# A conditioned transformer block on one core: gate vectors formed as columns and spread later, the last tile's output in three pieces, and a new order of all work

## The chip, the cores and the metric

The kernel runs on one core of a Trainium2 chip. A core has five engines with an instruction queue each: TensorE (PE, matmuls and transposes, writing to PSUM), VectorE (DVE), ScalarE (ACT), GpSimd (POOL) and SyncE (SP, which here issues DMAs). Each takes its instructions in the order in which they were written; between engines, semaphores hold an instruction back until its inputs are there. The metric is device time in microseconds (us), the median over runs of the whole program.

## What is computed

The block has an attention half A and a feed-forward half B. A conditioning vector `c` gives six modulation vectors of 512 numbers each: shifts `sa`, `sb`, scales `ca`, `cb` and gates `ga`, `gb`.

```python
mod = (_silu(c) @ w_mod).reshape(c.shape[0], 6, 1, -1)
sa, ca, ga, sb, cb, gb = (mod[:, 0], mod[:, 1], mod[:, 2], mod[:, 3], mod[:, 4], mod[:, 5])
h = _layernorm(x, axis=-1) * (1 + ca) + sa
x = x + ga * _A_ref(h, A_wqkv, A_w_phi, A_wo)
h = _layernorm(x, axis=-1) * (1 + cb) + sb
x = x + gb * _B_ref(h, B_w_gate, B_w_up, B_w_down)
```

`x` is 2048 tokens of 512 numbers in bf16. `_A_ref` is linear attention with 32 heads of width 16: q and k go through a small matrix per head, and `softmax(p)` and `softmax(-p)` side by side are the features; keys and values are summed to one small matrix per head, and each query reads it. `_B_ref` is `(silu(x @ w_gate) * (x @ w_up)) @ w_down` with a width of 1376.

## The kernel before

The tokens are 16 tiles of 128, in four chunks of four tiles. The work runs in these stages, which overlap:

- **Start.** SP loads x chunk by chunk and the weights. DVE takes layernorm statistics (`bn_stats`, line 348). The key weight is folded with the head matrices: PE transposes it (519), ACT copies the result from PSUM (523), PE multiplies (530) with the block matrix `BD` (made by DVE, 502), and ACT or DVE copy the folded weight back (533, 534). The shift and scale columns `modA` come from one-column matmuls against `w_mod` (473).
- **Keys and values.** Normalized tiles `xn` are turned to columns and modulated to `hT`. Tiles 0 to 5 are turned by PE (563, 414) with ACT or DVE modulating from PSUM (566, 567, 422); from tile 6 on by a DMA transpose into `raw` (577, called raw10 and raw11 by buffer), with POOL, ACT or DVE modulating (587, 589). For each tile, `k_tile` has PE compute k (619) and v (623), ACT exponentiate (634), DVE sum (640), and POOL multiply the second half of the features (657). `kv_tile` accumulates keys against values in PSUM (663). After the last one, DVE writes the matrix `KVZ`.
- **Queries.** `q_tile`: PE (686), ACT exponentials (690), DVE sums (694), POOL products (697, 701), and a DMA transpose into `pT` (705).
- **Attention.** `attend_tile` reads `pT` against `KVZ` (806), DVE divides (809, 810), a transpose gives `oT` (829 by DMA), `project` multiplies with `wo` (839), DVE adds to x (842), and the second layernorm follows: POOL (359 to 362), normalize, a DMA transpose into `raw` (853), and modulation to `hT` by DVE, ACT or POOL (860, 862, 864).
- **Feed-forward.** It runs in units of 1, 1, 2, 4, 4 and 4 tiles: gate and up products (891), silu on ACT (898), the product on DVE (901) or through ACT and POOL (905, 907), a narrow tail of 96 features (937 to 946), and `ffn_down` (969). The down product is multiplied by `gb` (980), added to x (984) and sent out by SP (989).

The gates `ga` and `gb` must stand as rows, the same on all 128 partitions, in `gab`. `gate` makes them in one step: for each quarter of the conditioning vector, PE takes one column of `silu(c)`, broadcast to 128 columns, as the stationary operand and streams 512 columns of `w_mod` (718); ACT copies the result from PSUM (721). `ga` is multiplied into `wo` by POOL (762). The variable `turned` marks the place from which the buffers of the first half may be used anew; it waits for `gab`, among others, and the first `attend_tile` waits for it.

The last tile's output is made in two halves of 256 columns. The first goes the usual way. The second uses `wdg`, the down weight with `gb` already multiplied in (916), so that after PE only one DVE operation (976) and the output DMA, which ACT issues, remain.

Nothing in this order is left to a scheduler. Every piece of work is recorded by `pl.op` with the engines that may do it, a duration for planning, and what it reads and writes. `ORDER` is a list written out by hand: each number is four times the number of an operation plus the choice of its engine. `Plan.run` goes through this list, works out a planned start for each operation from the durations, and issues all instructions sorted by that start. Where PE would be without work in the plan, `fill` puts in matmuls of ones whose result nobody reads (1036). `Plan.DMA` holds the plan's constants for DMAs; its last is the planned time from the end of a DMA transpose's transfer until its data count as there. Buffers in PSUM are six banks, given out in the planned order.

Of the kernel before, what the change touches and what calls it, by code (L numbers as in the profile page):

```python
# [7 lines left out]
BF16 = mybir.dt.bfloat16  # L8
FP32 = mybir.dt.float32
ACT = mybir.ActivationFunctionType  # L10
# [4 lines left out]
P = 128  # L15
# [5 lines left out]
D = 512  # L21
# [14 lines left out]
def fm_size(m):  # L36
# [10 lines left out]
    0, 4, 80, 72, 8, 12, 16, 48, 228, 188, 60, 204, 76, 20, 84, 89, 52, 220, 64, 192, 172, 208, 224, 232, 156, 160, 196, 164, 92, 56, 98, 236, 201,  # L47
    240, 244, 176, 212, 104, 108, 24, 100, 112, 248, 168, 216, 180, 116, 120, 148, 184, 153, 124, 132, 128, 276, 260, 28, 268, 40, 316, 272, 136,
    140, 280, 144, 324, 252, 520, 68, 488, 36, 285, 256, 424, 320, 328, 264, 288, 294, 298, 428, 524, 472, 464, 560, 600, 308, 432, 32, 476, 532,
    332, 564, 336, 300, 342, 44, 528, 480, 436, 468, 312, 608, 492, 368, 346, 484, 497, 380, 440, 445, 304, 568, 536, 541, 452, 604, 448, 572, 404,  # L50
    460, 500, 768, 372, 456, 548, 544, 612, 348, 556, 577, 376, 776, 392, 510, 584, 864, 408, 772, 358, 396, 617, 353, 366, 828, 780, 624, 832, 804,
    412, 812, 400, 820, 596, 362, 808, 552, 620, 416, 580, 513, 785, 792, 872, 904, 384, 636, 506, 518, 1004, 816, 824, 592, 388, 868, 876, 940,
    1008, 944, 836, 588, 640, 908, 704, 840, 708, 1012, 788, 912, 644, 632, 797, 1016, 648, 880, 860, 420, 628, 800, 916, 858, 712, 958, 900, 962,
    988, 950, 1044, 1021, 953, 888, 921, 853, 850, 1292, 1028, 736, 892, 716, 928, 740, 1024, 924, 964, 884, 846, 1172, 1288, 1312, 1328, 1176,
    1212, 652, 1216, 896, 720, 933, 1252, 656, 936, 1184, 1256, 1040, 744, 1220, 1344, 1180, 1224, 660, 1036, 1264, 664, 1189, 1336, 992, 1192,
    1229, 1196, 1297, 1320, 1260, 1208, 1302, 1236, 1032, 1306, 1309, 1340, 748, 1204, 1348, 1248, 1504, 1269, 1232, 1800, 1544, 1508, 1272, 1241,
    1276, 1244, 1201, 1353, 1584, 1588, 1356, 1281, 752, 1332, 1360, 968, 1592, 1516, 1284, 724, 1596, 1368, 1548, 1556, 1624, 972, 1372, 1512,
    1521, 1052, 1365, 668, 1552, 1524, 1528, 1540, 756, 1628, 976, 1536, 1601, 1636, 1561, 728, 1533, 980, 1604, 1580, 1641, 1608, 1048, 1108, 1564,
    1613, 1316, 1632, 1568, 1648, 1056, 1116, 1620, 1112, 1616, 1076, 1573, 672, 1644, 1576, 1660, 1808, 1653, 1120, 1080, 1656, 760, 676, 1812,
    1816, 996, 984, 680, 684, 732, 1000, 1324, 1820, 1728, 1840, 1844, 1084, 1060, 1736, 1848, 1088, 1092, 1664, 1140, 2148, 2152, 2156, 1796, 1672,  # L60
    1804, 1792, 1732, 1148, 1064, 1852, 764, 1856, 688, 1144, 1068, 1376, 1096, 1860, 1100, 2160, 1072, 1760, 1864, 2164, 1380, 1696, 1668, 1104,
    2168, 1868, 1764, 1472, 1872, 2400, 1700, 1440, 1152, 2404, 692, 1768, 2408, 1384, 1480, 1476, 696, 1408, 1876, 2412, 2172, 1882, 1704, 1124,
    1128, 2416, 1156, 1160, 700, 1884, 1892, 2200, 2420, 1896, 1164, 1888, 2176, 1132, 2204, 1996, 2208, 1920, 2180, 2212, 2424, 2184, 2216, 1444,
    2188, 1940, 1448, 1416, 2192, 1412, 2000, 1136, 1900, 1388, 2004, 2221, 1948, 1928, 1936, 1956, 1964, 1924, 1168, 2428, 1944, 2198, 1420, 2496,
    2008, 1932, 2224, 2452, 2012, 1960, 1952, 1904, 2237, 1424, 2500, 2016, 2504, 1428, 1908, 2432, 1392, 2508, 2456, 2242, 2020, 2436, 1484, 2440,
    2230, 1972, 2024, 2028, 1976, 2233, 2320, 2268, 1432, 1436, 2328, 2264, 2032, 2512, 2300, 1912, 2516, 1772, 2272, 1396, 2280, 2460, 2920, 1968,
    2037, 2316, 2336, 2288, 2324, 1488, 1400, 2284, 1916, 2520, 2924, 2276, 2040, 1776, 2292, 1492, 2308, 1980, 1496, 1404, 2548, 2044, 2244, 2048,
    2332, 1500, 1708, 2928, 2464, 2344, 2444, 1712, 2552, 2052, 2248, 2908, 2468, 2252, 2912, 2340, 2072, 2524, 2474, 1452, 2256, 1456, 2556, 2108,
    2088, 2916, 2449, 2560, 1984, 2296, 2564, 2528, 2116, 2932, 1460, 2476, 2112, 2092, 2120, 2376, 3016, 2532, 1465, 2076, 2100, 1468, 2536, 1676,
    2348, 3020, 2260, 2540, 2569, 1716, 2304, 2080, 1680, 2056, 2312, 2545, 2060, 2490, 3024, 2096, 2352, 1720, 1740, 2936, 2482, 2960, 2064, 3004,  # L70
# [50 lines left out]

class Plan:


    HOP = {"PE": 0.23, "DVE": 0.18, "ACT": 0.2, "POOL": 0.14, "SP": 0.0, "XBAR": 0.08, "NONE": 0.0}
    OWN = {"PE": 0.0, "DVE": 0.14, "ACT": 0.16, "POOL": 0.12, "SP": 0.0, "XBAR": 0.0, "NONE": 0.0}
    DMA = (1.7, 385e3, 0.5, 0.6, 1.15, 0.8)
    LANES = 8

    def __init__(self, slots):  # L130
        self.ops = []
        self.slots = slots
        self.queue, self.sent = 0.7, [2.5]
# [942 lines left out]
```

## Time and profile before

| quantity | value |
|---|---|
| time, median of 3 runs | 200.48 us (200.48 to 200.94) |
| the profiled execution | 200.42 us, of which the span of the profile is 198.6 us |
| granted TensorE clock | 1.00 |
| PE busy in the span | 193.3 us, 1450 matmuls |
| filler matmuls (L1036) | 25, all before 16 us |
| gate matmuls (L718) | 8 of 512 columns, the first at 30.5 us, the last group at 53.9 us |
| copies to gab (L721) | 2 of 0.576 us mean, at 38.4 and 54.8 us |
| first attend group (L806) | 55.59 us |
| DMA transposes, issue to landing, median | pT 3.3, raw 3.2, oT 3.3, gut 2.3 us |

PE is called busy from a matmul's start to its modelled end, so a busy PE can hide short waits; the starts of matmuls that follow each other are the better measure. A row of a timeline gives start, length, engine, line and operation, with idle time before it and what ended it in square brackets. A row of a group gives busy time and the mean of one. In the chain of waits each row is a stretch of the path that ended last. "issue" in it is time in which nothing that the profile shows was waited for.

### The profile page before, as it was taken

How to read it: one execution, taken by the hardware profiler on the slowest of the kernel's cores; microseconds unless marked ns; L12 is line 12 of the kernel's file. 1: busy time of each engine (PE TensorE's matmuls, PEld its weight loads, DVE VectorE, ACT ScalarE, POOL GpSimd, SP SyncE). 2: the span in 40 equal slices, each digit the busy share in tenths (PEclk: the TensorE clock that was granted, in tenths of full speed). 3: DMA queues.
4: the chain of work that ended last, by engine and by line, in shares of the span. 5: the costliest groups of instructions: out<-in, count | busy, mean ns of one | idle time of the engine just before them, and what ended most of it. 6: DMA issues, size and time to landing. Idle time of an engine off the chain costs nothing.

```text
span 198.6 us, 3986 instructions
## 1 busy us (share of the span) xinstructions
PE 193.3 (97%) x1450; PEld 107.4 (54%) x1450; DVE 138.2 (70%) x274; ACT 110.7 (56%) x243; POOL 122.5 (62%) x201
## 2 busy tenths in 40 slices
PE   7999999999999999999999999999999999999993
PEld 2755555456545776878644544544444454444542
DVE  4999999999999999979889728563305502214363
ACT  2799999998787973573334545454234444311200
POOL 1539999999997765783780487634272261962620
PEclk9999999999999999999999999999999999999999
DMA  6999877799798595544798333300311210020022
GB/s 203 345 392 142 237 121 213 177 360 314 183 194 165 109 154 31 112 80 59 144 189 80 71 68 79 83 0 13 79 27 42 79 53 0 13 70 1 26 92 66
DMA packets 50997, 24.16 MB, mean 122 GB/s; under 512 B 42177, under 2 KB 47778, under 8 KB 50978
## 3 DMA queue, kind: packets, MB, share of 16 engines
q1 hardware_dynamic: 50832, 23.85, 51.9%
q8 instruction: 11, 0.18, 0.4%
q10 hardware_dynamic: 146, 0.07, 0.1%
q14 instruction: 8, 0.07, 0.1%
HBM read 11.58 MB, written 2.10 MB: 69 GB/s over the span
## 4 chain that ended last, share of the span: by engine, by line
PE 84%; DMA 6%; POOL 3%; DVE 2%; SPq 1%; issue 1%; ACT 1%; DVEq 0%
PE one_ps L891 29%; PE one_ps L969 16%; PE one_ps L623 7%; PE one_ps L686 7%; PE one_ps L619 7%; PE one_ps L839 4%; PE kv_ps L1036 4%; DMA raw<-xn 3%; PE one_ps L937 2%; DMA pT<-eq 2%; PE kv_ps L663 2%; PE kv_ps L806 2%; PE one_ps L530 1%; PE one_ps L718 1%; PE one_ps L473 1%
## 5 line engine op out<-in xcount | busy, mean ns | idle before, releaser
L891 PE MATMUL one_ps<-hT,wgu_sb 128*128 128x512 bf16 (+2 forms) x480 | 74.5, 308 | 0.3 <-ACT hT L862 0.3
L891 PEld LDWEIGHTS <-wgu_sb 128*128 128x128 bf16 x480 | 39.9, 98 | 27.5 <-issue 0.6
L898 ACT ACTIVATE sg<-one_ps 128x512 bf16<-128x512 f32 (+1 forms) x41 | 23.5, 585 | 34.4 <-PE one_ps L891 31.4
L969 PE MATMUL one_ps<-wd_sb,gu 128*128 128x512 bf16 (+1 forms) x160 | 37.5, 372 | 0.0
L907 POOL TENSOR_TENSOR gu<-usb,sg 128x512 bf16<-128x512 bf16 x19 | 21.7, 1153 | 16.9 <-ACT sg L898 16.6
L980 DVE TENSOR_TENSOR fg<-one_ps,gab 128x512 bf16<-128x512 f32 (+1 forms) x16 | 10.7, 670 | 24.0 <-PE one_ps L969 24.0
L969 PEld LDWEIGHTS <-gu 128*128 128x128 bf16 x170 | 16.3, 98 | 16.8
L348 DVE BATCH_NORM_STATS2 st<-x_c 128x6 f32<-128x512 bf16 x32 | 20.9, 680 | 1.7 <-DMA x_c<-in_A_x_dram 1.7
L905 ACT CAST usb<-one_ps 128x512 bf16<-128x512 f32 x19 | 11.0, 583 | 16.1 <-PE one_ps L891 15.6
L901 DVE TENSOR_TENSOR gu<-one_ps,sg 128x512 bf16<-128x512 f32 (+1 forms) x22 | 14.3, 655 | 7.9 <-PE one_ps L891 5.4
L640 DVE TENSOR_REDUCE S<-e 128x64 f32<-128x1024 bf16 x16 | 19.0, 1204 | 0.3 <-POOL e L657 0.3
L694 DVE TENSOR_REDUCE Sq<-eq 128x64 f32<-128x1024 bf16 x16 | 19.1, 1199 | 0.0
L690 ACT ACTIVATE eq<-one_ps 128x512 bf16<-128x512 f32 x32 | 17.3, 608 | 1.5 <-PE one_ps L686 1.4
L984 POOL TENSOR_TENSOR ot<-x_c,fg 128x512 bf16<-128x512 bf16 x9 | 10.3, 1151 | 12.0 <-DVE fg L980 5.0
L657 POOL TENSOR_TENSOR e<-e,S 128x512 bf16<-128x512 bf16 x16 | 16.9, 1065 | 0.2
L634 ACT ACTIVATE e<-one_ps 128x512 bf16<-128x512 f32 x32 | 17.0, 600 | 0.0
L359 POOL TENSOR_SCALAR ln_neg<-ln 128x1 f32<-128x1 f32 x16 | 3.5, 220 | 20.7 <-DVE ln L349 20.1
L839 PE MATMUL one_ps<-wo_sb,oT 128*128 128x512 bf16 x64 | 15.8, 379 | 0.0
L619 PE MATMUL one_ps<-wk,hT 128*128 128x512 bf16 x64 | 15.4, 379 | 0.0
L623 PE MATMUL one_ps<-wv,hT 128*128 128x512 bf16 x64 | 15.4, 379 | 0.0
L686 PE MATMUL one_ps<-wq,hT 128*128 128x512 bf16 x64 | 15.3, 379 | 0.0
L701 POOL TENSOR_TENSOR eq<-eq,Rq 128x512 bf16<-128x512 bf16 x14 | 14.7, 1058 | 0.6
(117 smaller groups left out, 283.1 us busy)
## 6 DMA issues: line engine op xcount, KB each, us to landing
wmod_sb<-in_w_mod_dram SPq DMA_DIRECT2D x2, 1024.0 KB, 5.6
out_dram<-ot SPq DMA_DIRECT2D x15, 128.0 KB, 1.9
x_c<-in_A_x_dram SPq DMA_DIRECT2D x3, 512.0 KB, 7.5
wgu_sb<-in_B_w_up_dram SPq DMA_DIRECT2D x1, 1376.0 KB, 7.4
wgu_sb<-in_B_w_gate_dram SPq DMA_DIRECT2D x1, 1376.0 KB, 9.3
wd_sb<-in_B_w_down_dram SPq DMA_DIRECT2D x1, 1280.0 KB, 7.9
wk<-in_A_wqkv_dram SPq DMA_DIRECT2D x1, 512.0 KB, 4.5
wmod_sb<-in_w_mod_dram SPq DMA_DIRECT2D x1, 512.0 KB, 6.0
```

Source lines behind the costliest of these rows:

```text
L348: pl.op("DVE", r=reads, w=[st6], us=0.6, fn=lambda: nc.vector.bn_stats(st6()[:], src))
L619: nc.tensor.matmul(pk()[:], lhsT=hT[c_i][k][:, cols], rhs=Wk2[:, k, :], start=(k == 0), stop=(k == KD - 1))
L623: nc.tensor.matmul(v()[:], lhsT=hT[c_i][k][:, cols], rhs=wv_sb[:, k, :], start=(k == 0), stop=(k == KD - 1))
L640: pl.op("DVE", r=[e], w=[Ss], us=1.13, fn=lambda: nc.vector.tensor_reduce(Ss()[:].rearrange("p g s h -> p (g s h)"), e()[:].rearrange("p g ...
L686: nc.tensor.matmul(pq()[:], lhsT=hT[c_i][k][:, cols], rhs=Wq2[:, k, :], start=(k == 0), stop=(k == KD - 1))
L690: pl.op("ACT", r=[pq, btab], w=[be[sg]], us=0.48, fn=lambda sg=sg: nc.scalar.activation(eq[:, :, sg].rearrange("p g h f -> p g (h f)"), pq ...
L694: pl.op("DVE", r=be, w=[Sq], us=1.13, fn=lambda: nc.vector.tensor_reduce(Sq()[:].rearrange("p g s h -> p (g s h)"), eq[:].rearrange("p g s ...
L839: nc.tensor.matmul(a()[:], lhsT=oT()[:, j0 + j, :], rhs=wo_sb[:, j, :], start=(j == 0), stop=(j == KD - 1))
L891: nc.tensor.matmul(ps_()[0:fsz, q * n:(q + 1) * n], lhsT=wgu_sb[:, k, i, m * P:m * P + fsz], rhs=h2[k], start=(k == 0), stop=(k == KD - 1))
L898: pl.op("ACT", r=[g, btab], w=[sg], us=0.08 + 0.41 * L / CW, fn=lambda: nc.scalar.activation(sg()[0:fsz, 0:L], g()[0:fsz, 0:L], ACT.Silu))
L907: pl.op("POOL", r=[usb, sg], w=[gu], us=0.17 + 0.98 * L / CW, fn=lambda: nc.gpsimd.tensor_tensor(gu()[0:fsz, 0:L], usb()[0:fsz, 0:L], sg() ...
L969: nc.tensor.matmul(fp()[:], lhsT=b()[0:fsz, c0:c0 + P], rhs=wd_[0:fsz, m, wcs], start=(m == 0), stop=(m == FM - 1))
```

## The change

Four things change.

First, the gates are made in two steps. `gate` now makes each of its 512 numbers as a column: for each of four quarters of `c` and each of four blocks of 128 outputs, a one-column matmul with a block of `w_mod` as the stationary operand. The result is 128 partitions by 4 columns and is copied to `gcol`. `spread_gate` then makes the row form: each of four columns, broadcast to 128 columns, is the stationary operand, and the identity is streamed; the copy to `gab` follows, on ACT or DVE. `turned` waits for `gcol` instead of `gab`.

Second, the last tile's output is made in three pieces: 256, 128 and 128 columns. The second and third use `wdg`; SP sends the second and ACT the third.

Third, the plan's last DMA constant goes from 0.8 to 1.1.

Fourth, `ORDER` is a new list (the numbers of operations shift too, as there are more of them). With it, engines change for some operations: two of four WT copies (523) go from ACT to DVE, five normalizations from DVE to POOL, two from ACT to POOL and one from ACT to DVE, the statistics of chunk 2 from POOL to ACT, and others. On SP's queue, the loads of `wd` now stand before and between the transposes of chunk 2 and chunk 3 (raw11, raw10), and the second half of `w_mod` behind the latter. Lines after 712 move by 18.

```diff
 ORDER = [
-    0, 4, 80, 72, 8, 12, 16, 48, 228, 188, 60, 204, 76, 20, 84, 89, 52, 220, 64, 192, 172, 208, 224, 232, 156, 160, 196, 164, 92, 56, 98, 236, 201,
...
+    0, 4, 48, 188, 72, 80, 8, 12, 16, 76, 20, 60, 52, 204, 228, 84, 56, 220, 172, 64, 208, 89, 92, 98, 156, 232, 176, 224, 24, 212, 104, 180, 193,
...
-    DMA = (1.7, 385e3, 0.5, 0.6, 1.15, 0.8)
+    DMA = (1.7, 385e3, 0.5, 0.6, 1.15, 1.1)
...
+    gcol = const.tile([P, 2, KD], BF16, name="gcol")
+    bgcol = [Buf(), Buf()]
+
     def gate(gi):
-        col0 = (2 * D, 5 * D)[gi]
-        t = bank("fold")
+        n0 = (2 * KD, 5 * KD)[gi]
+        t = bank("fold", [P, KD])
 
         def f():
             for k in range(KD):
-                nc.tensor.matmul(t()[:], lhsT=silucT[:, k:k + 1].to_broadcast([P, P]), rhs=wmod_sb[:, k, col0:col0 + D],
-                                 start=(k == 0), stop=(k == KD - 1))
-        pl.op("PE", r=[bsil, bm2[gi]], w=[t], us=0.865, fn=f)
-        pl.op("ACT", r=[t], w=[bgab[gi]], us=0.49, fn=lambda: nc.scalar.copy(gab[:, gi, :], t()[:]))
+                for n in range(KD):
+                    nc.tensor.matmul(t()[:, n:n + 1], lhsT=wmod_sb[:, k, (n0 + n) * P:(n0 + n + 1) * P], rhs=silucT[:, k:k + 1],
+                                     start=(k == 0 and n == 0), stop=(k == KD - 1), skip_group_check=True)
+        pl.op("PE", r=[bsil, bm2[gi]], w=[t], us=0.42, fn=f)
+        pl.op([("DVE", 0.13, lambda: nc.vector.tensor_copy(gcol[:, gi, :], t()[:])),
+               ("ACT", 0.12, lambda: nc.scalar.copy(gcol[:, gi, :], t()[:]))], r=[t], w=[bgcol[gi]])
+
+    def spread_gate(gi):
+        t = bank("fold")
+
+        def f():
+            for n in range(KD):
+                nc.tensor.matmul(t()[:, n * P:(n + 1) * P], lhsT=gcol[:, gi, n:n + 1].to_broadcast([P, P]), rhs=ident_b[:],
+                                 start=True, stop=True)
+        pl.op("PE", r=[bgcol[gi]], w=[t], us=0.23, fn=f)
+        pl.op([("ACT", 0.49, lambda: nc.scalar.copy(gab[:, gi, :], t()[:])),
+               ("DVE", 0.6, lambda: nc.vector.tensor_copy(gab[:, gi, :], t()[:]))], r=[t], w=[bgab[gi]])
...
             gate(1)
+            spread_gate(0)
+            spread_gate(1)
...
-    turned = pl.op("NONE", r=bKVZ + bgab + [bmodB, bmodA] + bWq2, w=[bturn], us=0.0, fn=f_turn)
+    turned = pl.op("NONE", r=bKVZ + bgcol + [bmodB, bmodA] + bWq2, w=[bturn], us=0.0, fn=f_turn)
...
-        nh = 2 if n == NT - 1 else 1
-        for h in range(nh):
-            cs = slice(h * D // nh, (h + 1) * D // nh)
-            fp = bank("down", (P, D // nh))
+        pieces = [(0, D // 2), (D // 2, 3 * D // 4), (3 * D // 4, D)] if n == NT - 1 else [(0, D)]
+        for c0, c1 in pieces:
+            cs, cw, h = slice(c0, c1), c1 - c0, int(c0 > 0)
+            fp = bank("down", (P, cw))
...
-            q = nc.scalar if h == 1 else nc.sync
-            pl.op("ACT" if h == 1 else "XBAR", r=[ot], us=0.45, kb=-1,
+            on_act = c1 == D and h == 1
+            q = nc.scalar if on_act else nc.sync
+            pl.op("ACT" if on_act else "XBAR", r=[ot], us=0.45, kb=-1,
```

## The prediction

> **What bounds the kernel now.** I read the page's head first, then busy time by stretch, then the chain of waits, then the instructions of TensorE (PE) in order of time, and last the end of the run.
>
> ```profile
> span 198.6 us, 3986 instructions
> ...
> PE 193.3 (97%) x1450; PEld 107.4 (54%) x1450; DVE 138.2 (70%) x274; ACT 110.7 (56%) x243; POOL 122.5 (62%) x201
> ```
>
> PE is busy throughout, so the time is PE's own work plus what it loses. The loss has four places: the start, two waits in the middle, and the end. By stretch (columns: length, PE, weight loads, DVE, ACT, POOL, clock, DMA share, GB/s):
>
> ```profile
> 20.00:30.00 10.00, 10.00 (x75) 5.28 (x74) 10.00 (x20) 9.81 (x26) 9.92 (x19) 1.00 0.80 175
> 30.00:40.00 10.00, 10.00 (x75) 4.91 (x74) 9.95 (x13) 9.87 (x27) 9.78 (x17) 1.00 0.75 202
> 40.00:50.00 10.00, 10.00 (x117) 5.89 (x116) 9.65 (x12) 8.90 (x28) 10.00 (x19) 1.00 0.96 326
> ```
>
> From 20 to 50 us every engine is full: PE has no wait there, but whatever DVE, ACT or POOL deliver late would reach it at once. The two waits in PE's own timeline, and the links of the chain of waits in front of them:
>
> ```profile
> 77.00 4.53 PE L891 MATMUL one_ps<-hT,wgu_sb 128*128 128x256 bf16 x40
> 81.83 0.43 PE L806 MATMUL kv_ps<-KVZ,pT 128*128 128x68 bf16 x8 [0.30 <-DMA pT<-eq]
> ...
> 101.77 0.38 PE L891 MATMUL one_ps<-hT,wgu_sb 128*128 128x512 bf16 x1
> 102.43 0.81 PE L891 MATMUL one_ps<-hT,wgu_sb 128*128 128x512 bf16 x3 [0.28 <-ACT hT L862]
> ```
>
> ```profile
> 71.91 3.25 DMA raw<-xn
> ...
> 77.39 4.40 DMA pT<-eq
> ...
> 97.48 3.29 DMA raw<-xn
> 100.80 1.59 ACT hT L862 x3
> ```
>
> Matmul ends are modelled, so I price these two by starts. A 256-column matmul takes 0.108 us in a run (40 make 4.33), so L806 was due at 81.33 and began at 81.83: 0.50 lost. A 512-column one takes 0.2155 (0.86 for four in the chain), so from 98.74, fourteen of L969 and one of L891 end at 101.98; the next began at 102.43: 0.45. Together 0.95 us. The end:
>
> ```profile
> 195.29 0.33 SPq L989 DMA_DIRECT2D out_dram<-ot  x1
> 195.38 0.42 DVE L976 TENSOR_TENSOR ot<-one_ps,x_c 128x256 bf16<-128x256 f32 x1
> 195.83 0.38 ACTq L989 DMA_DIRECT2D out_dram<-ot  x1
> ```
>
> PE ends about 195.33, DVE at 195.80; the ACT piece lands 1.7 us after its issue (197.5), SP's last tile 1.9 after its own (197.2).
>
> **What the Trainium skill says.** "TensorE: Matmul & The Clock Gate", section "Wait — 56ns, not 53.3ns?", puts a floor of about 25 ns under start-to-start of small matmuls; here sixteen one-column L473 take 0.38 us in the chain and twenty-four 0.68, 24 to 28 ns each: it agrees. "DMA: Bandwidth & Descriptors", "Queues, rings and completion order", says that an SDMA engine takes the descriptors of a row in ring order, so a transpose issued behind a large load waits for it. The trace is consistent: SP's transposes and loads all sit on queue q1, and none is shown overtaking. "VectorE: DVE Perf Modes", "The perf-mode tier table", caps a copy out of PSUM at 2x; no row of before has DVE copying bf16 out of PSUM.
>
> **The change, part by part.**
>
> *Gates.* Two groups of four 512-column matmuls (L718) go: 2 x 0.86 = -1.72. Thirty-two one-column matmuls at 26 ns come: +0.83. Two spreads of four 128-column matmuls (0.22 per four, L414 in the chain): +0.44. Sum -0.45 on PE, which is the bound. Beside it come two tiny copies to gcol, bounded by nothing and by the 0.17 us of the modA copy (L478), on an ACT that also loses two WT copies; the gab copies stay (0.576 each). The turn no longer waits for gab: in before L806's first group began at 55.59, after gab ended at about 55.38, so that wait was already no stall. Worth zero.
>
> *Last tile.* Its second half becomes two 128-column pieces: 22 x 0.055 for 11 x 0.110, nothing on PE. At the end, DVE takes, in the new order, the multiply of tile 14's full width (ending about 0.5 before PE's end E), piece two (128 wide; about 0.28 against 0.42 for 256, as 0.14 of width goes), tile 14's full add (0.42), and piece three. With 0.05 of each overlapped, piece three starts at E+0.17 and ends at E+0.46; in before L976 ended at E+0.47. SP's copy of tile 14 goes behind piece two's copy (0.33 of SP): issue E+0.27, landing E+2.17; ACT's piece lands about E+2.15 against E+2.2. Gain 0 to 0.1; I take 0.
>
> *Fillers.* The built kernel has 26 instead of 25 fillers; by columns, 11842 instead of 11290: +552, at 512 per 0.2155 us +0.23.
>
> PE's instructions together: -0.45 + 0.23 = -0.22.
>
> *The start.* ACT gives two of four WT copies (L523, 0.57 each) to DVE, and POOL takes both halves of xn1; BD now stands behind four bn_stats and silu on DVE. By DVE's steps (0.627 per bn_stats, 0.56 for silu, 0.67 for BD) BD ends near 8.1 instead of 7.5. The two DVE copies I bound by 0.36 (2x) and 0.60 (1x, as 512 elements at the pace of L980). Either way ACT's three hT copies begin near 10.67 instead of 10.43 and the L422s end near 13.97 instead of 13.73. The first L619 comes near 12.2 (11.80 before), but 0.69 us less filler stands between the first and the fifth k or v tile. Counting all PE costs from the first instruction, the first L623 stands at 11.88 in the new order and would run at about 15.93; before, place 12.16 ran at 16.19. Lag 4.05 against 4.03: no gain, no loss; range -0.3 to +0.4.
>
> *20 to 45 us, the order.* The k tile that first reads hT_2 stands 1.14 us of PE work earlier (place 28.31, before 29.45), so it falls due near 32.4 rather than 33.5.
>
> ```profile
> 30.43 2.27 POOL L589 TENSOR_SCALAR hT<-raw,modA 128x512 bf16<-128x512 bf16 x3 [0.22 <-DMA raw<-xn]
> ```
>
> In before POOL ended its hT_2 share at 32.70, 0.8 before it was needed. In the new order the two raw11 transposes can be issued near 20.3 and 25.0 (the pair took 25.18 to 28.69), but POOL has two L657 (1.02 per step) among the three hT_2 pieces: adding POOL's steps I get 32.8, some 0.3 late. For k tile 6, all four hT_1 pieces now lie on POOL (0.53 each); they end near 24.85 against a need near 24.7. I take +0.35 for both, range 0 to +1.0. POOL's later work up to the last e has 1.1 us less than before (rstd of chunk 2 on ACT, two L653 gone, one hT piece more), so the last kv tile is not late.
>
> *The two waits.* For the first, PE work between the projection of tiles 2 and 3 and the waiting L806 was 14.44 us and becomes 15.64: +1.20, less 0.44 for two L697 that now stand before the eq product, leaves 0.76, above 0.50. For the second, PE work from the last projection of tiles 4 to 7 to their first gate group was 12.65 and becomes 15.18: +2.5 against 0.45. Both should go: -0.95, bounds 0 and -0.95. Next in line are chunk 2's hT (16.83 of PE work, before 19.70) and chunk 3's (16.64, before 25.73), with both under lighter engines; no charge.
>
> *One-column groups.* L473's four groups between 44 and 49 us cost about 0.3 beyond their count (an x8 took 0.29 for 0.19, the L623 behind it 0.89). Two more such groups and two spreads: +0.10, bounds 0 and 0.35.
>
> Sum: -0.22 + 0 + 0.35 - 0.95 + 0.10 + 0 = -0.72. The profiled execution took 200.42 (span 198.6 and 1.82 around it), 0.06 below the median of 200.48. So span 197.9, time 199.7.
>
> **Rivals.**
>
> *The waits only move.* For: DVE, POOL and SP run strictly in the written order, and the slack of chunk 3 shrinks by 9 us. Against: it still is above the 12.65 that nearly sufficed. Then -0.22 + 0.35 + 0.10 with 0.95 paid elsewhere less 0.3: 200.4.
>
> *Slower: the loads ahead of raw10.* The order puts wd (1280 KB) and half of w_mod (1024 KB) between the transposes of raw11 and those of raw10, in place of one 1024 KB load. One such load landed in 5.6 us; with some 1.9 of it fixed (an output tile of 128 KB), 2304 KB take 1.9 + 8.3 = 10.2, from about 26.5 to 36.7. Two transposes, issued near 32.5 and 35 and queued behind, land near 40 or, if each waits its turn, 42.3; hT_3 needs another 0.8 and is due near 41.2. It decides from a landing at 40.4 on, and costs up to 1.9; at 1.6 the time is 201.3.
>
> *Better.* The 0.35 of 20 to 45 us is hidden, DVE does the bf16 copies at the short bound (start -0.3), the end gives 0.1: 199.0.
>
> **Numbers.** Forecast 0.35, waits only move 0.25, loads 0.20, better 0.20. A measurement of this kernel tells 0.3% (0.60 us) from no change, so faster means below 199.88 and slower above 201.08. Of the forecast (199.3 to 200.1) four fifths are faster, with better that is 0.49; same is the rest of it and the second case, with a few of the loads: 0.31; slower 0.20. Range 199.0 to 201.2, for the unknown costs on both sides.
>
> **What would show it.** Right: L806 and L891 with no wait near 80 and 102, gate groups of 0.4 us in the chain, PE's end near 194.6. Wrong: PE waiting for hT (POOL) near 24 or 33, for hT_3 near 41, raw landing after 40.4, or new waits on raw after 115. A last piece ending clearly below 0.4 us after PE would correct my end.

## The result and the profile after

The changed kernel takes 199.28 us (median of 4 runs, 199.18 to 199.37). The kernel before took 200.71 us beside it (200.48 to 200.98). The ratio is 0.9928, with an interval from 0.9911 to 0.9946: faster by 0.7%. The profiled execution took 199.18 us, with a span of 197.4, against 200.42 and 198.6. The span fell by 1.2 us where the prediction had 0.72.

The page's head after, and busy time by stretch (length, PE, weight loads, DVE, ACT, POOL, clock, DMA share, GB/s):

```profile
span 197.4 us, 4080 instructions
...
PE 192.4 (97%) x1494; PEld 108.1 (55%) x1494; DVE 136.3 (69%) x268; ACT 108.9 (55%) x247; POOL 126.0 (64%) x207
```

```profile
20.00:30.00 10.00, 10.00 (x81) 5.44 (x79) 9.88 (x18) 9.87 (x26) 9.92 (x19) 1.00 0.77 172
30.00:40.00 10.00, 10.00 (x89) 5.34 (x88) 10.00 (x14) 9.87 (x28) 10.00 (x16) 1.00 1.04 272
40.00:50.00 10.00, 10.00 (x87) 5.20 (x84) 9.75 (x12) 9.74 (x31) 10.00 (x15) 1.00 1.09 355
```

From 20 to 50 us all engines are as full as before. That picture alone doesn't show a gain; the waits of PE do. First before, then after (what waited for what: us in total, times, longest):

```profile
PE kv_ps L1036 <- DVE ones L296: 1.4, 1, 1.4
PE kv_ps L806 <- DMA pT<-eq: 0.3, 1, 0.3
PE one_ps L891 <- ACT hT L862: 0.3, 1, 0.3
```

```profile
PE kv_ps L1054 <- DVE ones L296: 1.4, 1, 1.4
PE one_ps L519 <- DMA wk<-in_A_wqkv_dram: 0.4, 1, 0.4
```

The two waits in the middle are gone. What is left is before the first real product. In the chain of waits after (start, length, what) the two places where PE had stood still now follow PE's own work, and the gates are seen as groups of 0.38 (columns) and 0.22 us (spread):

```profile
37.41 0.38 PE one_ps L722 x16
...
51.85 0.38 PE one_ps L722 x16
...
64.32 0.22 PE one_ps L733 x4
...
79.04 3.49 PE one_ps L909 x32
82.53 0.25 PE kv_ps L824 x8
...
101.00 0.25 PE kv_ps L824 x8
101.25 2.81 PE one_ps L909 x13
```

To split the 1.2 us I price each matmul of PE by its pace in a run (0.2158 us for 512 columns, 0.1085 for 256, 0.056 for 128, 0.032 for 68, 0.024 for one) and add these up in PE's order, fillers included. The start that the trace shows, less that sum, is how far PE lags behind its own work. A lag that grows is a loss, wherever the profile books it.

| PE's lag, us, by time in the trace | before | after | growth before | growth after | difference |
|---|---|---|---|---|---|
| about 24 us, the start done | 3.87 | 4.12 | 3.87 | 4.12 | +0.25 |
| about 44 us | 4.04 | 4.13 | 0.17 | 0.01 | -0.16 |
| about 55 us, past the one-column groups | 4.25 | 4.36 | 0.21 | 0.23 | +0.02 |
| about 75 us | 4.51 | 4.59 | 0.26 | 0.23 | -0.03 |
| about 105 us, past the two waits | 5.49 | 4.64 | 0.98 | 0.05 | -0.93 |
| PE's last products | 5.53 | 4.69 | 0.04 | 0.05 | +0.01 |

The lag falls by 0.84. PE's own work falls by 0.25, from 189.58 to 189.33 (0.48 less for the gates, 0.23 more fillers). From PE's last product to the end of the span it is 3.18 us after 3.30, another 0.12. Together 1.21, which is what the span fell by (198.58 to 197.36).

### The profile page after: what moved, and what is told of

Its sections match the earlier page's. It is cut to its first block, busy times and chain, and to the rows that moved or that the text cites. A ratio compares the mean times of both kernels' runs of the same rounds, so it can differ in the third digit from the quotient of the medians.

```text
span 197.4 us, 4080 instructions
## 1 busy us (share of the span) xinstructions
PE 192.4 (97%) x1494; PEld 108.1 (55%) x1494; DVE 136.3 (69%) x268; ACT 108.9 (55%) x247; POOL 126.0 (64%) x207
## 4 chain that ended last, share of the span: by engine, by line
PE 93%; DMA 3%; DVE 1%; issue 1%; SPq 0%; DVEq 0%
PE one_ps L909 35%; PE one_ps L987 17%; PE one_ps L857 7%; PE one_ps L623 7%; PE one_ps L686 7%; PE one_ps L619 7%; PE one_ps L955 3%; DMA wk<-in_A_wqkv_dram 2%; PE kv_ps L663 2%; PE kv_ps L824 2%; PE kv_ps L1054 1%; DMA out_dram<-ot 1%; PE one_ps L530 1%; PE one_ps L473 1%; DVE fg L997 1%; PE one_ps L414 1%
## 5 line engine op out<-in xcount | busy, mean ns | idle before, releaser
L925 POOL TENSOR_TENSOR gu<-usb,sg 128x512 bf16<-128x512 bf16 x19 | 22.1, 1168 | 24.2 <-ACT sg L916 12.2
L623 PE MATMUL one_ps<-wv,hT 128*128 128x512 bf16 x64 | 15.9, 379 | 0.0
L619 PE MATMUL one_ps<-wk,hT 128*128 128x512 bf16 x64 | 15.5, 379 | 0.0
L1001 POOL TENSOR_TENSOR ot<-x_c,fg 128x512 bf16<-128x512 bf16 x7 | 8.1, 1153 | 10.0 <-DVE fg L997 10.0
L860 DVE TENSOR_TENSOR x_c<-x_c,one_ps 128x512 bf16<-128x512 bf16 x16 | 10.7, 669 | 5.3 <-PE one_ps L857 5.1
```

Of the source, the lines that this page charges most:

```text
L619: nc.tensor.matmul(pk()[:], lhsT=hT[c_i][k][:, cols], rhs=Wk2[:, k, :], start=(k == 0), stop=(k == KD - 1))
L623: nc.tensor.matmul(v()[:], lhsT=hT[c_i][k][:, cols], rhs=wv_sb[:, k, :], start=(k == 0), stop=(k == KD - 1))
L925: pl.op("POOL", r=[usb, sg], w=[gu], us=0.17 + 0.98 * L / CW, fn=lambda: nc.gpsimd.tensor_tensor(gu()[0:fsz, 0:L], usb()[0:fsz, 0:L], sg() ...
```

## The experiments

Each kernel was run beside the kernel before. The sessions' medians of before were 200.56, 200.52 and 200.57.

### Do the waits go by order alone?

The prediction said that both waits go because the new order puts more PE work ahead of them. The kernel before, with only two operations moved in `ORDER`, tests whether a little order is enough: the product that makes `eq` of tile 9 goes in front of an `hT` share on POOL, and SP's `gut` transpose goes behind the `raw` transpose that had waited for it.

```diff
-    2508, 2456, 2242, 2020, ... 2320, 2268, 1432, 1436, ... 3020, 2260, 2540, ... 3008, 2572, 1744,
+    2508, 2456, 1432, 2242, 2020, ... 2320, 2268, 1436, ... 3020, 2540, ... 3008, 2572, 2260, 1744,
```

> The kernel before with two moves in its order and nothing else: POOL's eq product (L701) of token tile 9 goes ahead of POOL's two hT pieces (L864), which stand waiting for raw until 75.25; and SP's raw transpose of tiles 6 and 7 goes ahead of the gut transpose that stood in front of it at 95.72. Theory (the two waits of PE are due to nothing but POOL's and SP's order): eq can run at 74.1 instead of 76.3, pT is issued near 75.2 instead of 77.4 and lands before 79, raw is issued near 96.0 instead of 97.5; both waits of PE (0.50 and 0.45) go, PE's lag behind the sum of its instructions stays near 4.5 from 76 us to the end instead of 5.5, 199.8 us, ratio to before 0.995. Rival (the waits only move): less than half of it arrives, 200.3 to 200.9, and the lag rises elsewhere.

Measured: 200.43 us, ratio 1.0001 (0.9986 to 1.0015). The lag no longer grows at the first wait (4.89 to 4.92), but at the second place it grows as much as ever, 4.95 to 5.49, for another reason. PE's wait there, and the chain:

```profile
PE one_ps L969 <- DMA gut<-gul: 0.4, 1, 0.4
```

```profile
97.57 2.88 DMA gut<-gul
...
100.49 0.40 PE one_ps L969
```

PE waits for `gut` instead of `hT`. Of two transposes that stand in a row on SP's queue, whichever goes second was late. This is the rival "the waits only move", made real. The execution that was profiled also started 0.3 us late.

The next kernel moves `gut` forward instead, right behind the operation that makes its input:

```diff
-    2508, 2456, 2242, ... 1452, 2256, 1456, ... 3020, 2260, 2540,
+    2508, 2456, 1432, 2242, ... 1452, 2256, 2260, 1456, ... 3020, 2540,
```

> The kernel before with two moves, the second another than in the run of two moves: POOL's eq product of token tile 9 goes ahead of POOL's two hT pieces as there, and on SP it is the gut transpose that goes forward, from 95.72 to where its input is ready (about 89.3, SP idle there), so that the raw transpose behind it can be issued when its xn is ready (95.95) and gut is not late either. Theory (both waits come from POOL's and SP's order and can be had without touching the gates): no wait of PE near 80 or 102, lag flat from 76 us to the end, 0.9 us of the profile's sum goes, 199.6 to 199.8 us, ratio 0.995 to 0.996. Rival (another wait takes their place, as gut did): a new step in the lag, 200.3 to 200.6 us.

Measured: 199.93 us, ratio 0.9965 (0.9950 to 0.9980), span 197.8. SP's rows (start, length, issue) before and here:

```profile
77.39 1.23 SPq L705 DMA_TRANSPOSE pT<-eq  x1
...
95.72 1.25 SPq L946 DMA_TRANSPOSE gut<-gul  x1
97.48 1.26 SPq L853 DMA_TRANSPOSE raw<-xn  x1
```

```profile
75.42 1.23 SPq L705 DMA_TRANSPOSE pT<-eq  x1
...
88.97 1.17 SPq L946 DMA_TRANSPOSE gut<-gul  x1
...
95.64 1.25 SPq L853 DMA_TRANSPOSE raw<-xn  x1
```

Both transposes that PE had waited for are issued about 1.9 us earlier, PE has no wait after the start, and its lag ends at 4.76, close to the changed kernel's 4.69. The lag grows by 0.03 and 0.01 at the two old places; about 0.1 comes back before them, so that the span is 0.8 us shorter and the time, by the ratio, 0.7. So most of the 0.95 could be had without touching a gate. The new order does the second the same way: its `raw` is issued at 94.14.

### The gates

The changed kernel with the gates in one step again: four matmuls of 512 columns each, and the wide copy where the narrow one stood. Order, tail and fillers' rule are those of the changed kernel; in place of the spread a one-column product, whose result nobody reads, keeps the place.

```diff
-                for n in range(KD):
-                    nc.tensor.matmul(t()[:, n:n + 1], lhsT=wmod_sb[:, k, (n0 + n) * P:(n0 + n + 1) * P], rhs=silucT[:, k:k + 1],
+                nc.tensor.matmul(t()[:], lhsT=silucT[:, k:k + 1].to_broadcast([P, P]), rhs=wmod_sb[:, k, n0 * P:n0 * P + D],
```

> The changed kernel with its order, its tail and its fillers, but the gates formed as before: four 512-column products each at the place of the one-column products, with the wide copy to gab there; one one-column product and a one-column copy stand at the place of each spread. Theory (PE is the bound there, so the gates are worth their instructions): +1.72 - 0.83 - 0.44 + 0.05 = +0.50 of PE against the changed kernel, no wait returns near 80 or 102, so 199.8 us, ratio to before 0.9953. Rival one (the short gates are what made the waits go): lag up by 0.5 to 0.95 besides, 200.3 to 200.7. Rival two (one-column products cost more than their count, and the wide copy on ACT hides): within 0.15 us of the changed kernel.

Measured: 200.71 us, ratio 1.0004 (0.9992 to 1.0016). The expected 199.8 us was missed. Relative to the changed kernel this is a loss of 1.43 us by the medians of two sessions, and of 1.2 by the two profiles (the profiled execution here, 200.34, was shorter than the median). PE's work is only 0.56 more (189.89 against 189.33). The rest is lag, which grew from 4.06 at 40 us of work to 5.21 at 70, against 4.13 to 4.58. Part of it is a wait that the change doesn't name, for `oT`. In the chain:

```profile
66.84 4.82 DMA oT<-o
...
71.71 0.39 PE one_ps L857
```

The same transpose took 3.0 us in the changed kernel. That difference needed a cause.

First, the wide copy: does it matter that it stands early, on the full engines? The changed kernel with the second gate's spread, and so its wide copy, moved to just behind `turned` (the copy starts at 56.0 instead of 68.1; with the old gates the two copies stood at 38.3 and 53.1):

```diff
-    1496, 1148, 1012, 1720, ... 1780, 2200, 1016, 2204,
+    984, 1680, 1836, ... 1812, 1864, 1012, 1156, 1104, 1016, 1108,
```

> The changed kernel with the second gate's spread and its wide copy to gab (ACT, 0.58 us) moved forward, from behind the q tiles (64.3 and later) to behind the turn (near 56), as early as gab was written in the kernel before; every engine's other instructions in the same order. PE's work is the same. Theory (the wide copy in ACT's crowded stretch from 50 to 66 us makes the last q tiles' eq, so oT, late; that is what the kernel with old gates lost beyond its products): lag 0.3 to 0.6 more by 72 us with PE waiting for oT near 71, 199.6 to 199.9 us. Rival (the old gates lost by PE's own later place): lag as in the changed kernel, 199.2 to 199.4 us.

Measured: 199.47 us, ratio 0.9945 (0.9924 to 0.9966). The lag grows by 0.52 from 40 to 75 us of work, in the changed kernel by 0.46. So the place of the second copy, as far as this run moves it, isn't the cause; an earlier place, and the first copy's, were not tried.

Then the new gates alone, in the kernel before with its own order (the rule that would add fillers after the start is set to none, so that the fillers are those of before):

```diff
-    turned = pl.op("NONE", r=bKVZ + bgab + [bmodB, bmodA] + bWq2, w=[bturn], us=0.0, fn=f_turn)
+    turned = pl.op("NONE", r=bKVZ + bgcol + [bmodB, bmodA] + bWq2, w=[bturn], us=0.0, fn=f_turn)
...
+            spread_gate(0)
+            spread_gate(1)
```

> The kernel before with nothing of the change but the gates: one-column products and a small copy at the old places, spread of gate 0 near 45 us and of gate 1 near 65 us as in the changed kernel, the turn waiting for the columns; order, fillers and tail as before. Theory (gates are worth their instructions, the waits belong to the order): -0.45 of PE, both waits near 82 and 102 stay, 200.0 to 200.25 us, ratio 0.9978. Rival one (the gates with the late copy also make room on ACT, and the waits go): 199.2 to 199.5 us, ratio 0.994. Rival two (the waits swallow it: PE comes to them earlier and waits longer, so nothing is left): 200.5 us and waits longer by 0.3 to 0.45.

Measured: 201.01 us with much scatter (200.01 to 202.65), ratio 1.0024 (0.9997 to 1.0051). The gain of 0.48 in PE's work doesn't show. The first wait is gone, though nothing in SP's order changed (lag 6.00 to 6.02). The second became 1.6 us. The chain there:

```profile
97.30 5.13 DMA raw<-xn
...
102.46 1.59 ACT hT L880 x3
```

The same transpose, from the same place on the same queue, took 3.29 us before. This profile is of one of the longer executions (202.02 us); three took 200.01 to 200.13, as expected for gates worth their instructions, and no trace shows what differed in them.

### What makes a transpose take 5 us instead of 3

On the page's part 3 (queue, kind: packets, MB, share of 16 engines' span) there is a queue besides the kernel's own. It brings instructions:

```profile
q8 instruction: 11, 0.18, 0.4%
```

That is 16 KB a packet. In the trace the eleven took 0.9 to 1.4 us each, 1.1 in the mean. They come once per about 250 instructions of PE (186 to 340 lie between two in before), within a few tens of the same PE instruction in every kernel. So a change in the number of PE's instructions shifts all later packets in time: the changed kernel has 88 more of them (2988 against 2900). The DMA view for the stretch from 77.3 to 81.8 us, where `pT` is on its way; first before, then the gates alone:

```profile
q1 hardware_dynamic: 1214, 0.30, 71.1%
q8 instruction: 1, 0.02, 1.9%
```

```profile
q1 hardware_dynamic: 1184, 0.30, 33.4%
```

The kernel's queue q1 moves the same 0.30 MB, but with a q8 packet beside it its packets take 0.711 x 16 x 4.5 / 1214 = 42 ns each, without it 20. The reader sees a delay that belongs to no line of the kernel. Over the kernels (packet times to 0.25 us):

| transpose, kernel | issued | q8 packet from | landed after |
|---|---|---|---|
| pT, before | 77.39 | 78.7 | 4.40 |
| raw, before | 97.48 | none | 3.29 |
| oT, after | 66.16 | 66.2 | 3.0 |
| oT, old gates | 66.84 | 69.7 | 4.82 |
| raw, gates alone | 97.30 | 100.2 | 5.13 |

In this table a packet that starts between 1.1 and 3.0 us after the issue goes with a landing in 4.4 to 5.1 us instead of 3.0 to 3.4, and one at the issue does nothing. Over all transposes of `pT`, `oT` and `raw` after 60 us in the fourteen traces it is a strong rule, not a strict one. In 43 flights a packet began 1.0 to 3.0 us after the issue: 37 landed in 3.8 to 5.1 us, and six, with the packet at 2.5 us or later, in 3.0 to 3.1 (one is `oT` of the changed kernel, issued at 87.31). Of 260 with no q8 packet from 1.5 us before the issue to 3.3 after it, 252 landed within 3.6 us. The other eight, in 4.1 to 4.3, all have in their flight a packet of q14, a second instruction queue with packets of 8 KB; sixteen other flights with such a packet were not late. The test is to shift the packets and nothing else: the kernel before, with each of its early fillers cut into four pieces, so that PE's instructions are more while its order, and that of all other engines, stays. (The four pieces together have 3/4 of the columns.)

```diff
-                fns.append(lambda n=min(left, CW): f(n))
+                n = min(left, CW)
+                fns += [lambda n=n: f(n)] if t0 >= 7.0 else [lambda n=n * 3 // 16: f(n)] * 4
```

> The kernel before, with eleven of the filler products of the first 6 us cut into four of three sixteenths of the columns each: 66 more instructions of PE, no more work, every order unchanged. In the trace of before a packet of queue q8 (0.18 MB in 11 packets: instructions being fetched) starts near 69.2, 78.7 and 107.2, inside the flight of the three transposes that land in 4.8, 4.4 and 4.6 us instead of 3.0 to 3.4; by PE's count of instructions these packets come every 210 to 270 instructions. Theory (the fetch for PE holds up a transpose in flight, and the first wait of before, on pT, is 1.1 us of fetch): 66 instructions move the packet at 78.7 to about 75.6, pT issued at 77.39 lands in 3.1 to 3.4 and PE's first wait (0.50) goes, the second stays; 200.0 to 200.1 us, ratio 0.9975. Rival (chance, or another engine's fetch): pT lands in 4.4 as before, the wait stays, 200.5 us.

Measured: 201.62 us, ratio 0.9994 (0.9971 to 1.0018); the expected 200.0 to 200.1 was missed. The median can't be used, for the start was slow too (as shown for the next kernel), and the profiled execution, 202.54, was one of the longer ones, so only landings are read. (Six of the 22 executions, 199.17 to 199.83, were shorter than every one of before beside it, 199.95; none of them was profiled.) `pT`, issued at 78.69, landed in 3.1 us, and the first wait was gone (lag 6.31 to 6.35). The late start gave it no more room: PE reached its product at 82.67, 3.98 us after the issue, against 3.94 in before. The packet that had met `pT` came at 76.6, ahead of its issue; a later one, at 107.1 in before, came at 100.2 and met `raw`, and the second wait became 1.4 us. The DMA view for 97.6 to 102.5 us, and the chain:

```profile
q8 instruction: 1, 0.02, 1.8%
...
raw<-xn SPq DMA_TRANSPOSE x1, 4.9
```

```profile
97.62 4.94 DMA raw<-xn
```

So which transpose is slow follows the packet, not the order. The same cut in the kernel with the old gates asks whether the late `oT` was the packet's:

> The kernel with the changed order and the old gates (g_old_gates), with the early fillers cut as in the first run of this set: 66 more instructions of PE, as many again as the old gates had taken away. There oT, issued at 66.84, landed in 4.8 us with a q8 packet at 69.7 in its flight, and PE waited for it near 71.7. Theory (fetch): oT lands in 3.0 to 3.4, no wait near 71.7, lag at 70 us 4.6 to 4.9 instead of 5.2, 200.0 to 200.3 us; what is left against the changed kernel is the 0.5 of instructions and what PE's later place costs on ACT. Rival (the gates' wide copy or place makes oT late): lag and time as in g_old_gates, 200.7 us.

Measured: 201.42 us, ratio 1.0036 (1.0017 to 1.0055). `oT` landed in 3.3 us, PE didn't wait for it (from issue to due time it had 4.4 us in both kernels), and the lag grew by 0.70 from 40 to 75 us of work, where the old gates had lost 1.15 to 70. So of the old gates' 1.2 us in the profiles 0.56 is PE's work and about 0.45 the packet. Some 0.2 of lag, and the other 0.2 by which the medians differ, stay without a cause. The time rose at the start, where the lag reached 6.19 instead of 4.12 (0.6 of that are only the columns cut from the fillers, a quarter of eleven times 0.2158). PE's timeline, here and in the changed kernel:

```profile
6.63 1.44 PE L519 MATMUL one_ps<-ident_b,wk 128*128 128x128 bf16 x12
7.87 1.49 PE L1054 MATMUL kv_ps<-ones 128*128 128x512 bf16 x3
```

```profile
6.70 0.83 PE L519 MATMUL one_ps<-ident_b,wk 128*128 128x128 bf16 x12
7.36 0.81 PE L1054 MATMUL kv_ps<-ones 128*128 128x512 bf16 x3
```

By the starts of the two rows twelve matmuls took 1.24 us here and 0.66 there. The array ran at about half its pace.

Two more kernels put the new gates into the old order with shifted packets (fillers cut into five), without and with the two moves that took both waits away.

```diff
-                fns.append(lambda n=min(left, CW): f(n))
+                n = min(left, CW)
+                fns += [lambda n=n: f(n)] if t0 >= 7.0 else [lambda n=n * 3 // 20: f(n)] * 5
```

> The kernel with the gates alone (g_gates_alone) with the early fillers cut into five each: 88 more instructions of PE, no more work. There raw, issued at 97.30, landed in 5.1 us with a q8 packet at 100.2 in its flight, and the times scatter from 200.0 to 202.7. Theory (fetch): the packet comes near 96.3, raw lands in 3.1 to 3.5, PE's wait near 102 falls from about 1.6 to 0.4 to 0.9, median 200.0 to 200.4 us and less scatter. Rival (the gates alone make raw late by order or by engines): raw still in 5 us or issued later, 201.0 us.

> The kernel before with its own tail and order, and three things together: the gates as columns (as in g_gates_alone), the two moves of w_gut_early, and the early fillers cut into five each. Theory (each keeps its worth once the waits are out of the way: -0.8 for the moves, -0.45 for the gates, fetch out of flight): no wait of PE after the start, 199.2 to 199.5 us, ratio 0.994, level with the changed kernel, without its order and without three pieces. Rival (the waits come back elsewhere as the gates bring PE forward): 199.9 us or more with a new step in the lag.

Measured: 204.31 us, ratio 1.0179 (1.0155 to 1.0202), without the moves; 203.61 us, ratio 1.0147 (1.0126 to 1.0167), with them. Three parts that each look good alone did not add up. With the moves, PE's lag does pass the first old wait unharmed and the second with 0.3 (9.49 at 70 us of work, 9.54 at 85, 9.84 at 100), but by then it has grown by 0.9 between 35 and 40 us of work and by 1.5 between 55 and 60, where PE waits 1.3 us for a `pT`; and its start was at half pace. Without the moves, the start was at full pace, and the losses are 1.3 and 1.4 in the same two stretches, 0.7 for a `WT` transpose, and 0.7 at the second old wait. There the `pT` issued at 60.96 landed in 4.95, with a packet near 63.75. So a shift of the packets rescues one transpose and hits another; and in the gates alone, too, the old order lost 0.9 between 25 and 35 us of work, which it had not lost without the new gates. What delays PE there with the gates in the old order was not found.

### Fillers and tail

The prediction charged the extra fillers in full. The changed kernel without any filler planned after 7 us:

```diff
-FILL_FROM, FILL_TO, FILL = 1.3, 90.0, 0.85
+FILL_FROM, FILL_TO, FILL = 1.3, 7.0, 0.85
```

> The changed kernel without the fifteen filler products that stand after the first 7 us of the plan (2.8 us of PE); nothing else. The prediction counted fillers as work on the bound. Theory A (they only fill time in which PE would wait): PE starts its first L619 at the same 12.35, the lag behind the real work is unchanged at 20 us, 199.3 us. Theory B (they push PE): first L619 near 11.5, second group of L619 bounded by ACT's L422 ending 13.84, so the first L623 comes 0.3 to 0.9 us earlier; what of it reaches the end depends on DVE, ACT and POOL, which are full from 20 to 50 us: 198.5 to 199.1 us, or PE waits for hT between 20 and 45 us and nothing is left. Theory C (the clock falls without them): a granted clock under 1.00 before 20 us, and slower than the changed kernel.

Measured: 199.04 us (198.97 to 199.46), ratio 0.9939 (0.9921 to 0.9958), level with the changed kernel's 0.9928 (0.9911 to 0.9946). 2.78 us of fillers are gone and at most some 0.2 us of time. PE's timeline shows where they had lain:

```profile
12.22 3.28 PE L619 MATMUL one_ps<-wk,hT 128*128 128x512 bf16 x14 [0.63 <-ACT hT L566]
15.89 1.02 PE L623 MATMUL one_ps<-wv,hT 128*128 128x512 bf16 x4 [0.39 <-DMA wv<-in_A_wqkv_dram]
```

PE waits for `hT` and `wv` where it had run fillers, and the first `L623` comes at 15.89 instead of 15.99 (both by the timeline). Fillers at the start fill waits; counting their columns as time is wrong.

At the end of the changed kernel the last DVE operation starts 0.18 us after PE's last product, because its output buffer is the one from which tile 13 is still being sent. The chain after:

```profile
192.29 1.96 DMA out_dram<-ot
...
194.28 0.05 DVEq L993
194.33 0.04 issue
194.37 0.29 DVE ot L993
```

A fourth buffer should take this wait away:

```diff
-             "usb": 2, "ot": 3, "fg": 3}
+             "usb": 2, "ot": 4, "fg": 3}
```

> The changed kernel with four ot buffers instead of three, PE's order the same. In the changed kernel's chain the last piece's add waits for an output to land (192.29 + 1.96 = 194.25) and starts at 194.37, while the last product ends near 194.2. Theory (that buffer sets the last add): the add starts 0.05 to 0.1 us earlier against PE's last product, and the chain at the end goes back to PE; 199.2 us. Rival (DVE's tile-14 add, which ends at 194.22, or PE sets it): no change in the distance from PE's last product to the add, 199.3 us, chain through DVE.

Measured: 199.39 us (198.98 to 199.93), ratio 0.9950 (0.9931 to 0.9969). The addition now starts 0.11 after PE's last product instead of 0.18, so the wait was there. But the end came no sooner: from that product to the end it is 3.19 us after 3.18, as ACT's last output took 1.79 us to land instead of 1.70. No gain is shown.

Last, two pieces instead of three, also with four buffers:

```diff
-        pieces = [(0, D // 2), (D // 2, 3 * D // 4), (3 * D // 4, D)] if n == NT - 1 else [(0, D)]
+        pieces = [(0, D // 2), (D // 2, D)] if n == NT - 1 else [(0, D)]
```

> The kernel with four ot buffers (t_four_ot) with the last tile in two halves as in the kernel before, tile 14's add ahead of the second half's. Theory (three pieces are worth 0 to 0.1 us): the last add starts 0.05 to 0.1 after PE's last product and takes 0.42 instead of 0.29, and PE's last product is as late; 199.3 to 199.5 us. Rival (the short last piece is worth the shorter add and the shorter output, 0.13 and more): 199.5 to 199.8 us.

Measured: 199.93 us (199.58 to 201.22), ratio 0.9963 (0.9947 to 0.9979). DVE's timeline:

```profile
194.35 0.42 DVE L993 TENSOR_TENSOR ot<-one_ps,x_c 128x256 bf16<-128x256 f32 x1 [0.18 <-PE one_ps L987]
194.69 0.41 DVE L1001 TENSOR_TENSOR ot<-x_c,fg 128x512 bf16<-128x512 bf16 x1
```

Tile 14's addition (L1001) ran behind the last piece here, not ahead of it, so SP's last output went late: 3.72 us from PE's last product to the end, where two halves in the old order took 3.30 (before) and 3.28 (`gut` early). So the order of these two additions is worth about 0.4 us. The run doesn't price the third piece. That comes from the same two kernels, against 3.18 to 3.21 for three pieces (the changed kernel, without fillers, and second spread early): 0.1.

No kernel of these is faster than the changed one by more than the intervals.

## Why the prediction was right

| term | predicted | measured |
|---|---|---|
| PE's instructions: gates -0.45, fillers +0.23 | -0.22 | -0.25 |
| start | 0 | +0.25 |
| order, 20 to 45 us | +0.35 | -0.16 |
| one-column groups | +0.10 | +0.02 |
| two waits | -0.95 | -0.93 |
| tail | 0 | -0.12 |
| sum | -0.72 | -1.21 (with -0.02 elsewhere) |

The time of 199.28 against the predicted 199.7 lies within the range. The two terms that carry the gain, the gates and the waits, hold to 0.03 us each. The difference is in the terms that were bounded rather than read. Two of these missed in opposite directions, the order by -0.51 and the start by +0.25, so the total came nearer than its parts.

**Gates.** The price by rows held: the column group takes 0.38 and the spread 0.22 in the chain, and PE's work fell by 0.48. No run shows the 0.48 as time by itself: it is a count of instructions at their pace, and in the old order the new gates alone gained nothing by the median. That the run with one-step gates lost 1.2 in the profiles (1.43 by medians) is not the gates' price either: 0.45 of it was a transpose that met an instruction packet.

**Two waits.** The size is right; the reason was not complete. The prediction counted PE work between producer and consumer. In the trace the first wait needed two things at once: an issue of `pT` 3.94 us before its due time of 81.33, and a packet that made it land in 4.40 instead of about 3.2. A shifted packet is enough (fetch shift), and so are two microseconds of order (`gut` early), which also brought `pT` down, in 3.1 us, before the packet came. The changed kernel has a little of both:

```profile
78.03 1.23 SPq L705 DMA_TRANSPOSE pT<-eq  x1
```

```profile
82.37 0.42 PE L824 MATMUL kv_ps<-KVZ,pT 128*128 128x68 bf16 x8
```

From issue to use it is 4.34 us, 0.40 more than before, where the prediction had counted on 0.76, because the issue moved back too, by 0.64. With a flight of 4.40 that would have left some 0.1 us of the wait. But no packet came in between (76.0 and 89.8 are the nearest), and `pT` landed in 3.2. That the packet moved away, with the number of PE's instructions, was luck: the prediction knew nothing of it. The second wait was order: `raw` stood behind `gut` on SP.

**Order, 20 to 45 us.** This is the step that failed, by its size: +0.35 for an `hT_2` 0.3 us late. POOL's last share of hT_2 ended at 32.44, where I had added up 32.8, and PE's groups follow one another without idle time there:

```profile
31.56 1.03 PE L623 MATMUL one_ps<-wv,hT 128*128 128x512 bf16 x4
32.42 1.03 PE L619 MATMUL one_ps<-wk,hT 128*128 128x512 bf16 x4
33.29 0.67 PE L663 MATMUL kv_ps<-va,e 128*128 128x68 bf16 x16
```

hT_1 ended at 24.6, before its need near 24.7. The kernel before, on the other hand, did lose 0.17 in this stretch, which I hadn't seen.

**Start.** Zero predicted, +0.25 in the two profiles, inside the bounds. The pieces came as worked out: BD ended at 7.88 (8.1 predicted); by the chain, the first `L619` came at 12.35 (12.2) and the first `L623` at 16.05 (15.93). But the start differs between executions of kernels that are the same up to there (lag 3.87 to 4.22 with the old order; the last section shows from what), so this term stays open. Nor do the fillers' 0.23 stand on their own, as the run without them shows.

**One-column groups.** Two groups and two spreads more cost +0.02 in lag; the 0.10 was within its bounds.

**Tail.** The predicted addition in 0.28 took 0.29, and the new order of additions came as described. The gain of 0.12 is at the upper bound of 0.1; I took the lower. The sign that I gave, a last piece ending clearly below 0.4 us after PE, did not come: PE ended at 194.19 and the piece at 194.66, 0.47 later, of which the buffer's wait is part.

**Rivals.** "The waits only move" is false for this change, and true for the two moves; with the gates alone, in the profiled execution, the first wait went and the second grew. "The loads ahead of raw10" is false: the two loads had landed by 35.6 us (36.7 estimated), the two transposes, issued at 32.31 and 34.62, by 36.5 and 37.7, and POOL began on hT_3 at 38.86, 1.5 us before the landing of 40.4 from which that rival decides. "Better" (199.0) named the right places, the order and the end, and the time fell between it and the forecast.

## What to carry to other kernels

When a wait on a DMA transpose is short, look at how far its issue stands ahead of its use, and at whether an instruction packet lies in its flight, before explaining it by the work around it; leave 5 us, not 3, where a kernel of some thousand instructions must not wait. Split a gain into PE's own work and PE's lag along the span: a change in the count of instructions can move a delay from one transpose to the next, so one part of a change, run alone, may show a loss that isn't its own. Fillers that lie in waits cost nothing, and shortening them where they keep PE busy at the start can cost the array's pace.

## What was not expected of the hardware

**Instruction packets delay transposes.** Packets of 16 KB, about 1.1 us each, come once per some 250 PE instructions. Of the 43 transposes after 60 us with one beginning 1.0 to 3.0 us into their flight, 37 landed in 3.8 to 5.1 us, where the usual is 3.0 to 3.4. The Trainium skill, "DMA: Bandwidth & Descriptors", section "Queues, rings and completion order", says that each DMA engine goes round its queues a packet at a time, and that a completion's semaphore lands only after every earlier write of that engine, across its queues. This fits a transpose that is complete only when the engine with the instruction packet is through. That this is the mechanism no run shows, nor why six flights escaped.

**The pace of the array at the start is partly a matter of chance.** The two kernels with fillers cut into five have the same instructions on PE up to 10 us. Their timelines, without the two moves and with them:

```profile
5.80 0.40 PE L519 MATMUL one_ps<-ident_b,wk 128*128 128x128 bf16 x4 [0.62 <-DMA wk<-in_A_wqkv_dram]
...
6.70 0.83 PE L519 MATMUL one_ps<-ident_b,wk 128*128 128x128 bf16 x12
```

```profile
5.83 0.61 PE L519 MATMUL one_ps<-ident_b,wk 128*128 128x128 bf16 x4 [0.60 <-DMA wk<-in_A_wqkv_dram]
...
6.70 1.44 PE L519 MATMUL one_ps<-ident_b,wk 128*128 128x128 bf16 x12
```

The same gap of 0.6 us, and one execution goes on at full pace, the other at half. Of four kernels with shortened early fillers three were at half pace in their profile. In the other kernels the first four of L519 took 0.39 to 0.41 us in before, after and four more, and 0.51 to 0.63 in four, in one of which (four buffers) the next twelve were slow in part as well, 1.13. Those four started 0.2 to 0.5 later; a fifth (second spread early) started 0.3 later and waited for `wv` instead. The granted clock in these profiles stays at 0.997 or above and shows none of this. The page "TensorE: Matmul & The Clock Gate", section "What's actually happening", says that the array is released by about 3.4 us of activity, judged in a window that runs freely, so that "the same kernel measures 6, 11, or 14 cold-MMs"; the section after it gives 106.7 ns for 128 columns before and 55.6 after. The traces agree: start to start, the matmuls of 128 columns in the slow groups stand 106 to 107 ns apart and those of the profile at full pace 55 to 57, and the start differs from run to run. Why short fillers meet the slow pace more often, no run here shows.
